# A value path on unscaled rows for the first block of a spectral filter with a gated MLP

## The chip, the cores and the metric

The kernel runs on one core of one Trainium2 chip. The metric is the device time of one execution in microseconds. Before the change, the median of 5 runs is 895.74 us (894.26 to 896.88).

## The reference

```python
def _attn_ref(x, filt_r, filt_i):          # x: 8 x 3008 x 256
    X = np.fft.rfft(x, axis=1)
    Y = X * (filt_r + 1j * filt_i)[None]
    return np.fft.irfft(Y, n=x.shape[1], axis=1)

def _moe_ref(x, w_gate, w_val, w_out, rms_g):   # x: 24064 x 256, hidden width 1536
    rms = np.sqrt(np.mean(x * x, axis=-1, keepdims=True) + 1e-06)
    xn = x / rms * rms_g
    g = xn @ w_gate
    silu = g * (1.0 / (1.0 + np.exp(-g)))
    return silu * (xn @ w_val) @ w_out
```

The first function filters each of the 8 sequences along its length in the frequency domain. The second normalizes every row of the result by its root mean square, multiplies by a gain for each column, and puts it through a gated MLP. Inputs and output are fp32. Row scaling and a matmul on the columns commute: `(x / rms * g) @ w` is `((x * g) @ w) / rms`. That holds for the value product and for the output product, not for the gate, which goes through a nonlinear function.

## The kernel before, in words

The transforms are matmuls with constant tables, in two stages forward and two back. Sequence 0 has its own set-up path (lines 637 to 734), which keeps everything on the chip; sequences 1 to 7 go through DRAM scratch tensors and are interleaved with the MLP of the sequence before.

The MLP works in blocks of 512 rows: 6 blocks for each of 8 sequences, and for each block 12 steps over the hidden width in slices of 128. One step is a slot. `gv` (line 429) runs four 128x512 matmuls: two halves of the contraction (dt 0 and 1) for the gate into `pg`, two for the value into `pv`. ScalarE makes `sg`, the Silu of `pg`; VectorE multiplies `pv` by it into `hh`. `down`, two slots later, multiplies `hh` by the output weights and accumulates in two PSUM banks, `po0` and `po1`. After the last slice ScalarE copies `po0` and VectorE copies `po1` to the output tile `o3` (lines 465 and 466), which is then stored. `pg` and `pv` have two PSUM buffers each.

The normalized rows `xn` of a block come from a chain. `n_first` (block (0,0)) or `n_unit` (the others) makes the last transform stage `psn`, transposed so that the 256 columns lie in two halves of 128 partitions; `dh` 0 and 1 name the halves. ScalarE squares both into `sq`. `y` is `psn` times the gain: for block (0,0), `y_first` does half 0 on VectorE and half 1 on ScalarE. `q_unit` sums the squares by matmuls with a vector of ones into `psq`; VectorE makes `u` (line 353), and GpSimd raises it to the power -0.5 into `rho`, one number a row. For block (0,0) `scale_split` splits `rho` into two fp16 parts `hl`, and `scale_apply` spreads them over the partitions by matmuls (`psr`) and multiplies `y` by them into `xn` on VectorE, half after half.

Every engine gets its instructions in the order in which the program writes them down, so what waits holds up all that stands behind it on its engine. From line 753 on, a list of slots with functions planned into them is such an order for the whole MLP. Around the change the order is written out by hand:

```python
        first = n_first()
        t2_unit(3, 1, 1)
        t2_unit(4, 1)
        t2_unit(5, 1)
        fill = bank(2, "pw")
        warm_up(2, fill)
        y_first(*first, 1)
        q_unit(0, 0)
        t2_unit(6, 0, 0)
        t2_unit(7, 0)
        warm_up(5, fill)
        y_first(*first, 0)
        scale_split(0, 0)
        scale_apply(0, 0, 3)
```

`t2_unit(j, eng)` is four transposes of data of sequence 0 and their copy out of PSUM, on VectorE where `eng` is 1 and on ScalarE where it is 0; the PSUM bank is shared with the unit two before it where no other is given. `warm_up` runs 128x512 matmuls on zeros whose result nobody reads. `bank(1, ..)` and `bank(2, ..)` take the next buffer of `pg` and of `pv`. The weights are loaded by `w_load` in three parts on GpSimd's queue, two in line 706 and on, the third after the set-up (line 732), ahead of the loads of sequence 1.

Of the kernel before, what the change touches and what calls it, by code (L numbers as in the profile page):

```python
# [10 lines left out]
FP32 = mybir.dt.float32  # L11
FP16 = mybir.dt.float16
AXT = mybir.ActivationFunctionType
ALU = mybir.AluOpType
# [6 lines left out]
P = 128  # L21
# [100 lines left out]
def kernel(  # L122
# [11 lines left out]
    nc = tc.nc  # L134
# [9 lines left out]
    glob = ctx.enter_context(tc.tile_pool(name="glob", bufs=1))  # L144
# [6 lines left out]
    up = ctx.enter_context(tc.tile_pool(name="up", bufs=2))  # L151
    xnp = ctx.enter_context(tc.tile_pool(name="xnp", bufs=4))
    hp = ctx.enter_context(tc.tile_pool(name="hp", bufs=4))
    psG = ctx.enter_context(tc.tile_pool(name="psG", bufs=2, space=bass.MemoryType.PSUM))
    psV = ctx.enter_context(tc.tile_pool(name="psV", bufs=2, space=bass.MemoryType.PSUM))
# [11 lines left out]
    wg = glob.tile([P, 2, DFF], FP16)  # L167
    wv = glob.tile([P, 2, DFF], FP16)
    wo = glob.tile([P, JT, D], FP16)
    gsb = glob.tile([P, 2], FP32)  # L170
    hhs = [glob.tile([P, 512], FP16, name="hh%d" % i) for i in range(4)]
    ones = glob.tile([P, 1], FP16)
    mhalf = glob.tile([P, 4], FP32)


    st = {b: {"x": {}, "t1": {}, "t2": {}, "s": {}, "t3": {}, "t4": {}, "y": {}, "sq": {},
# [14 lines left out]
    def bank(i, name):  # L191

        pool, tag = ((psM, "mx"), (psG, "pg"), (psV, "pv"), (psB, "mb"), (psO, "po1"), (psO, "po0"))[i]
        return pool.tile([P, 512], FP32, tag=tag, name=name)
# [114 lines left out]
    def nq(b, m):  # L309
        return 3 if (m == 5 and b % 2 == 0) else 4  # L310
# [24 lines left out]
    def halved(b, m):  # L335
        return b > 1 and (b, m) != (2, 0)
# [5 lines left out]
    def q_unit(b, m):  # L342
        sq = st[b]["sq"].pop(m)
        ps = bank(1, "psq")
        n = nq(b, m)
        parts = 1 if halved(b, m) else 2
        for q in range(n):
            for dh in range(parts):
                nc.tensor.matmul(ps[:, q:q + 1], sq[:, dh, ts(q, P)], ones,  # L349
                                 start=(dh == 0), stop=(dh == parts - 1))  # L350
        u = up.tile([P, 4], FP32, tag="u", name="u")
        rho = up.tile([P, 4], FP32, tag="rho", name="rho")
        nc.vector.tensor_scalar(out=u[:, 0:n], in0=ps[:, 0:n], scalar1=1.0 / D, scalar2=1e-6 * Y_SCALE * Y_SCALE,  # L353
                                op0=ALU.mult, op1=ALU.add)
        nc.gpsimd.tensor_tensor(out=rho[:, 0:n], in0=u[:, 0:n], in1=mhalf[:, 0:n], op=ALU.pow)  # L355
        if (b, m) not in by_matmul:
            nc.gpsimd.dma_start(r_d[b, m, 0:n * P].rearrange("(p q) -> p q", q=n), rho[:, 0:n])
        else:
            st[b]["u"][m] = rho
# [7 lines left out]
    def n_first():  # L367

        y = yp.tile([P, 2, 512], FP32, tag="y", name="y")
        sq = sqp.tile([P, 2, 512], FP16, tag="sq", name="sq")  # L370
        pss = [bank(1 + dh, "psn") for dh in range(2)]
        for dh in range(2):
            for q in range(4):
                nc.tensor.matmul(pss[dh][:, ts(q, P)], st[0]["t4"][0][:, q, ds(dh * P, P)], wai,
                                 start=True, stop=True)
            nc.scalar.activation(out=sq[:, dh, :], in_=pss[dh], func=AXT.Square)
        st[0]["sq"][0] = sq
        st[0]["y"][0] = y
        return y, pss

    def y_first(y, pss, dh):
        if dh:
            nc.scalar.activation(out=y[:, dh, :], in_=pss[dh], func=AXT.Identity, scale=gsb[:, dh:dh + 1])
            return
        nc.vector.tensor_scalar(out=y[:, dh, :], in0=pss[dh], scalar1=gsb[:, dh:dh + 1],
                                scalar2=None, op0=ALU.mult)

    def scale_split(b, m):
        rho = st[b]["u"].pop(m)
        hl = up.tile([P, 2, 4], FP16, tag="hl", name="hl")  # L390
        nc.vector.tensor_copy(out=hl[:, 0, :], in_=rho)
        nc.vector.tensor_tensor(out=hl[:, 1, :], in0=rho, in1=hl[:, 0, :], op=ALU.subtract)
        st[b]["u"][m] = hl
# [26 lines left out]

    by_matmul = ((0, 0), (0, 1), (1, 0))
    hh_of = {}
    po_of = {}
    late_p = {}

    def cut(b, m, part):
        return (0, nq(b, m)) if part is None else (2 * part, 2)

    def gv(b, m, jt, part):
        q0, n = cut(b, m, part)  # L430
        w = n * P
        xn = st[b]["xn"][m][:, :, q0 * P:q0 * P + w]
        pg = psG.tile([P, 512], FP32, tag="pg", name="pg")
        pv = psV.tile([P, 512], FP32, tag="pv", name="pv")
        order = [(e, dt_) for e in range(2) for dt_ in range(2)]
        if (b, m, jt) == (0, 0, 0):
            order = [(e, dt_) for dt_ in range(2) for e in range(2)]
        for e, dt_ in order:
            ps, wt = ((pg, wg), (pv, wv))[e]
            nc.tensor.matmul(ps[:, 0:w], wt[:, dt_, ts(jt, P)], xn[:, dt_, :],  # L440
                             start=(dt_ == 0), stop=(dt_ == 1))
        sg = hp.tile([P, 512], FP16, tag="sg", name="sg")
        hh = hhs[(6 * JT * b + JT * (m + (part or 0)) + jt) % 4]
        nc.scalar.activation(out=sg[:, 0:w], in_=pg[:, 0:w], func=AXT.Silu)  # L444
        nc.vector.tensor_tensor(out=hh[:, 0:w], in0=pv[:, 0:w], in1=sg[:, 0:w], op=ALU.mult)  # L445
        hh_of[(b, m, jt, part)] = hh

    def down(b, m, jt, part):
        hh = hh_of.pop((b, m, jt, part))
        if jt == 0:  # L450
            where = {None: ((psO, "po0"), (psO, "po1")), 0: ((psO, "po0"),), 1: ((psO, "po1"), (psM, "mx"))}
            po_of[(b, m, part)] = [pool.tile([P, 2, D], FP32, tag=tag, name=tag)
                                   for pool, tag in where[part]]
        po = po_of[(b, m, part)]

        n = cut(b, m, part)[1]
        per = 1 if part else 2
        for s4 in range(n):
            nc.tensor.matmul(po[s4 // per][:, s4 % per, :], hh[:, ts(s4, P)], wo[:, jt, :],  # L459
                             start=(jt == 0 and s4 % per == 0),  # L460
                             stop=(jt == JT - 1 and (s4 % per == per - 1 or s4 == n - 1)))
        if jt == JT - 1:
            o3 = late_p["op"].tile([P, 4, D], FP32, tag="o3", name="o3")
            if part is None:
                nc.scalar.activation(out=o3[:, 0:2, :], in_=po[0], func=AXT.Copy)
                nc.vector.tensor_copy(out=o3[:, 2:n, :], in_=po[1][:, 0:n - 2, :])  # L466
            else:
                nc.scalar.activation(out=o3[:, 0, :], in_=po[0][:, 0, :], func=AXT.Copy)
                nc.vector.tensor_copy(out=o3[:, 1, :], in_=po[part][:, 1 - part, :])
            po_of[(b, m, part)] = o3  # L470
# [105 lines left out]
    def t2_unit(j, eng, bk=None):  # L576
        c, r = divmod(2 * j, XC)
        if r == 0:
            st[0]["t4"][c] = t4p.tile([P, XC, D], FP16, tag="t4", name="t4")
        pool, tag = (psO, "po%d" % (j % 2)) if bk is None else ((psM, "mx"), (psB, "mb"))[bk]  # L580
        ps = pool.tile([P, 2, D], FP16, tag=tag, name="pt2")
        for a in range(2):
            for dh in range(2):
                src = gT[:, dh, :].rearrange("p (i n) -> p n i", n=H)[:, 2 * j + a, :]
                nc.tensor.transpose(ps[:, a, ts(dh, P)], src, ident)  # L585
        dst = st[0]["t4"][c][:, r:r + 2, :]
        if eng:
            nc.vector.tensor_copy(out=dst, in_=ps)
        else:
            nc.scalar.activation(out=dst, in_=ps, func=AXT.Copy)  # L590
# [20 lines left out]
    def warm_up(n, pw):  # L611
        if isinstance(pw, int):
            pw = bank(pw, "pw")
        for i in range(n):
            nc.tensor.matmul(pw, wz[:, 0:P], wz, start=True, stop=True)
# [5 lines left out]

    def w_load(q):
        cols = ts(q, DFF // 3)
        for src, dst in ((moe_w_gate, wg), (moe_w_val, wv)):
            nc.gpsimd.dma_start(dst[:, :, cols], src.rearrange("(dt p) j -> p dt j", p=P)[:, :, cols])
        nc.gpsimd.dma_start(wo[:, ts(q, JT // 3), :],
                            moe_w_out.rearrange("(jt p) d -> p jt d", p=P)[:, ts(q, JT // 3), :])

    with tc.manual_schedule():
# [84 lines left out]
        t2_unit(2, 1, 0)  # L714
        first = n_first()
        t2_unit(3, 1, 1)
        t2_unit(4, 1)
        t2_unit(5, 1)
        fill = bank(2, "pw")
        warm_up(2, fill)  # L720
        y_first(*first, 1)
        q_unit(0, 0)
        t2_unit(6, 0, 0)
        t2_unit(7, 0)
        warm_up(5, fill)
        y_first(*first, 0)
        scale_split(0, 0)
        scale_apply(0, 0, 3)
        t2_unit(8, 0)
# [147 lines left out]
```

## Time and profile before

| what | value |
|---|---|
| median of 5 runs | 895.74 us (894.26 to 896.88) |
| the profiled execution | 893.84 us, span of its instructions 892.1 us |
| TensorE busy | 874.7 us (98%), granted clock 1.00 |
| VectorE, ScalarE, GpSimd busy | 677.2, 623.9, 428.6 us |
| first gate matmul | 47.74 us after the span's start |
| last slice of block (0,0) accumulated, copies begin | 69.92 us |

The median belongs to plain runs, the rows of the profile to one profiled execution, which has a time of its own. Busy time of TensorE is counted to the modelled end of each matmul, and neighbours overlap, so a busy TensorE may still have small waits in it. In a timeline a row gives the start, the length, the engine, the line of the kernel and what is written from what; rows of one kind that follow each other are merged.

### The profile page before, as it was taken

To read this page: it belongs to the slowest core of one execution; us is meant where nothing else is said; L and a number is where in the kernel's file an instruction comes from. 1 tells how busy PE (TensorE), PEld (TensorE's weight loads), DVE (VectorE), ACT (ScalarE), POOL (GpSimd) and SP (SyncE) were. 2 spreads that over 40 slices of the span, in tenths; PEclk is the share of its full clock that TensorE was granted. 3 is DMA by queue.
4 is the path that set the end of the run, shared out by engine and by line. 5 is a ranking of instruction groups with operands and counts; after the bars stand their busy time and mean duration, and the time that the engine had idled before them with its cause. 6 is when DMAs were issued, how large, how long until landed. Compare 5 with 4: busy or idle time off the path is not lost.

```text
span 892.1 us, 17504 instructions
## 1 busy us (share of the span) xinstructions
PE 874.7 (98%) x6289; PEld 561.3 (63%) x6289; DVE 677.2 (76%) x1085; ACT 623.9 (70%) x1063; POOL 428.6 (48%) x385
## 2 busy tenths in 40 slices
PE   8799999999999999999999999999999999999997
PEld 5666666666666666666666666666666666666556
DVE  7866766889988887888688786888878887555555
ACT  7877666677677766877677766787657765676444
POOL 7843720656437652577236662376515762155300
PEclk9999999999999999999999999999999999999999
DMA  9595826674653446434645347332352232221301
GB/s 199 109 205 155 157 61 202 142 161 114 155 159 98 101 101 186 116 86 117 152 125 127 87 84 199 80 103 83 84 165 72 66 89 60 87 67 48 72 24 48
DMA packets 80094, 101.43 MB, mean 114 GB/s; under 512 B 8108, under 2 KB 56684, under 8 KB 79560
## 3 DMA queue, kind: packets, MB, share of 16 engines
q1 hardware_dynamic: 69688, 84.23, 34.6%
q0 software_dynamic: 10240, 15.96, 11.2%
q8 instruction: 49, 0.80, 0.4%
q14 instruction: 37, 0.30, 0.1%
q10 hardware_dynamic: 80, 0.13, 0.1%
HBM read 67.67 MB, written 46.78 MB: 128 GB/s over the span
## 4 chain that ended last, share of the span: by engine, by line
PE 91%; DVE 3%; issue 2%; POOL 1%; DMA 1%; ACT 1%; POOLq 0%; DVEq 0%
PE po L459 27%; PE pg L440 26%; PE pv L440 26%; PE psb L238 3%; PE psi L288 3%; PE psn L320 2%; PE psa L203 2%; DMA xc<-in_x_dram 1%; DVE o L466 1%; DVE hh L445 1%; PE psq L349 1%; POOL xc L188 0%; PE pt L546 0%; POOL xn L416 0%; PE pt L585 0%
## 5 line engine op out<-in xcount | busy, mean ns | idle before, releaser
L445 DVE TENSOR_TENSOR hh<-pv,sg 128x512 f16<-128x512 f32 (+2 forms) x588 | 393.3, 670 | 195.4 <-ACT sg L444 82.9
L444 ACT ACTIVATE sg<-pg 128x512 f16<-128x512 f32 (+2 forms) x588 | 341.0, 580 | 226.6 <-PE pg L440 217.8
L459 PE MATMUL po<-wo,hh 128*128 128x256 f16 x2244 | 343.1, 272 | 2.9 <-DVE o L466 2.2
L440 PE MATMUL pg<-xn,wg 128*128 128x512 f16 (+2 forms) x1176 | 339.6, 370 | 0.1
L440 PE MATMUL pv<-xn,wv 128*128 128x512 f16 (+2 forms) x1176 | 339.6, 370 | 0.0
L459 PEld LDWEIGHTS <-hh 128*128 128x128 f16 x2256 | 216.3, 98 | 98.0 <-issue 4.3
L279 POOL TENSOR_TENSOR s<-s,s 128x512 f16<-128x512 f16 x96 | 111.1, 1157 | 230.8 <-DVE s L273 159.6
L440 PEld LDWEIGHTS <-wv 128*128 128x128 f16 x1176 | 114.8, 98 | 128.8 <-issue 0.3
L416 POOL TENSOR_TENSOR xn<-y,rb 128x1024 f16<-128x1024 f32 (+1 forms) x45 | 126.1, 2803 | 44.0 <-DMA rb<-r_tmp 41.0
L440 PEld LDWEIGHTS <-wg 128*128 128x128 f16 x1176 | 111.3, 98 | 13.2 <-issue 0.6
L355 POOL TENSOR_TENSOR rho<-u,mhalf 128x4 f32<-128x4 f32 (+1 forms) x48 | 49.0, 1021 | 63.1 <-DVE u L353 62.6
L293 ACT ACTIVATE t<-psi 96x512 f16<-96x512 f32 x112 | 66.4, 593 | 9.4 <-PE psi L288 4.3
L326 ACT ACTIVATE y<-psn,gsb 128x512 f32<-128x512 f32 (+1 forms) x94 | 63.8, 679 | 8.1 <-PE psn L320 0.9
L273 DVE TENSOR_TENSOR s<-psb,fi 64x512 f16<-64x512 f32 x96 | 65.7, 684 | 3.0
L275 DVE SCALAR_TENSOR_TENSOR s<-psb,fi 64x512 f16<-64x512 f32 x96 | 66.5, 693 | 1.3
L249 DVE TENSOR_TENSOR s<-psb,fr 128x512 f16<-128x512 f32 x96 | 65.4, 681 | 0.0
L340 POOL TENSOR_TENSOR sq<-sq 128x512 f16<-128x512 f16 (+1 forms) x35 | 39.7, 1133 | 34.3 <-ACT sq L332 34.3
L332 ACT ACTIVATE sq<-psn 128x512 f16<-128x512 f32 (+1 forms) x94 | 54.8, 582 | 0.0
L208 ACT ACTIVATE t<-psa 128x512 f16<-128x512 f32 x70 | 41.8, 597 | 5.6 <-PE psa L203 2.4
L288 PE MATMUL psi<-s,wi 128*128 128x256 f16 x248 | 45.4, 273 | 0.0
L238 PE MATMUL psb<-t,wb 96*128 96x256 f16 x224 | 43.0, 272 | 0.7 <-DVE s L266 0.7
L320 PEld LDWEIGHTS <-t 128*128 128x128 f16 x368 | 28.4, 98 | 20.6 <-issue 0.4
(106 smaller groups left out, 533.6 us busy)
## 6 DMA issues: line engine op xcount, KB each, us to landing
out_dram<-o SPq DMA_DIRECT2D x83, 256.0 KB
xc<-in_x_dram POOLq DMA_DIRECT2D x56, 192.0 KB, 6.1
z_tmp<-t SPq DMA_DIRECT2D x28, 384.0 KB
t<-z_tmp SPq DMA_DIRECT2D x28, 384.0 KB
g_tmp<-t SPq DMA_DIRECT2D x56, 192.0 KB
rb<-r_tmp SPq DMA_DIRECT2D x41, 256.0 KB
t<-g_tmp SPq DMA_DIRECT2D x21, 384.0 KB
t<-g_tmp SPq DMA_DIRECT2D x7, 320.0 KB
```

The lines of the kernel that those rows point to most:

```text
L238: nc.tensor.matmul(ps[:, u, :], w[:, k, :], t, start=True, stop=True)
L249: nc.vector.tensor_tensor(out=s1, in0=ps, in1=f1, op=ALU.mult)
L273: nc.vector.tensor_tensor(out=s2[a], in0=ps[e], in1=f2[e], op=ALU.mult)
L275: nc.vector.scalar_tensor_tensor(out=s2[a], in0=ps[e], scalar=-1.0, in1=f2[e], op0=ALU.mult, op1=ALU.mult)
L279: nc.gpsimd.tensor_tensor(out=s, in0=s1, in1=s2, op=ALU.add)
L288: nc.tensor.matmul(ps[:, u, :], wi_at(q, 2 * i + u), ss[q][:, u, :], start=(q == 0), stop=(q == n - 1))
L293: nc.scalar.activation(out=st[b]["t3"][c][:, 2 * r:2 * r + 2, :], in_=ps[0:KR], func=AXT.Copy)
L416: nc.gpsimd.tensor_tensor(out=xv, in0=yv, in1=rv.unsqueeze(1).to_broadcast([P, 2, n, P]), op=ALU.mult)
L440: nc.tensor.matmul(ps[:, 0:w], wt[:, dt_, ts(jt, P)], xn[:, dt_, :], start=(dt_ == 0), stop=(dt_ == 1))
L444: nc.scalar.activation(out=sg[:, 0:w], in_=pg[:, 0:w], func=AXT.Silu)
L445: nc.vector.tensor_tensor(out=hh[:, 0:w], in0=pv[:, 0:w], in1=sg[:, 0:w], op=ALU.mult)
L459: nc.tensor.matmul(po[s4 // per][:, s4 % per, :], hh[:, ts(s4, P)], wo[:, jt, :], start=(jt == 0 and s4 % per == 0), stop=(jt == JT - 1 an ...
```

## The change

Block (0,0)'s value product is made from rows that carry the gain but not yet the row scale, in fp16 (`y16`). Its first two slices are multiplied ahead of the row scale, in the place of the warm-up matmuls. The gate still uses `xn`. The row scale `rho`, kept in a tile of its own, is applied where block (0,0)'s output leaves PSUM, in two operations of 256 columns on ScalarE and two on VectorE. The value weights are loaded before the gate weights.

```diff
-        rho = up.tile([P, 4], FP32, tag="rho", name="rho")
+        rho = up.tile([P, 4], FP32, tag="rho", name="rho") if (b, m) != (0, 0) else rho0
...
+        y16.append(xnp.tile([P, 2, 512], FP16, tag="xn", name="y16"))
...
+    def val_first(jt):
+        pv = psV.tile([P, 512], FP32, tag="pv", name="pv")
+        for dt_ in (1, 0):
+            nc.tensor.matmul(pv, wv[:, dt_, ts(jt, P)], y16[0][:, dt_, :], start=(dt_ == 1), stop=(dt_ == 0))
+        pv_of[jt] = pv
...
-        pv = psV.tile([P, 512], FP32, tag="pv", name="pv")
-        order = [(e, dt_) for e in range(2) for dt_ in range(2)]
-        if (b, m, jt) == (0, 0, 0):
-            order = [(e, dt_) for dt_ in range(2) for e in range(2)]
-        for e, dt_ in order:
-            ps, wt = ((pg, wg), (pv, wv))[e]
-            nc.tensor.matmul(ps[:, 0:w], wt[:, dt_, ts(jt, P)], xn[:, dt_, :],
-                             start=(dt_ == 0), stop=(dt_ == 1))
+        pv = pv_of.pop(jt) if (b, m) == (0, 0) and jt < 2 else None
+        if pv is None:
+            pv = psV.tile([P, 512], FP32, tag="pv", name="pv")
+            operands = ((pg, wg, xn), (pv, wv, y16[0] if (b, m) == (0, 0) else xn))
+        else:
+            operands = ((pg, wg, xn),)
+        for ps, wt, src in operands:
+            for dt_ in range(2):
+                nc.tensor.matmul(ps[:, 0:w], wt[:, dt_, ts(jt, P)], src[:, dt_, :],
+                                 start=(dt_ == 0), stop=(dt_ == 1))
...
-            if part is None:
+            if (b, m) == (0, 0):
+                for q in range(4):
+                    src = po[q // 2][:, q % 2, :]
+                    if q < 2:
+                        nc.scalar.activation(out=o3[:, q, :], in_=src, func=AXT.Copy, scale=rho0[:, q:q + 1])
+                    else:
+                        nc.vector.tensor_scalar(out=o3[:, q, :], in0=src, scalar1=rho0[:, q:q + 1],
+                                                scalar2=None, op0=ALU.mult)
+            elif part is None:
...
-        for src, dst in ((moe_w_gate, wg), (moe_w_val, wv)):
+        for src, dst in ((moe_w_val, wv), (moe_w_gate, wg)):
...
         t2_unit(3, 1, 1)
+        y_first(y16[0], first[1], 0)
         t2_unit(4, 1)
         t2_unit(5, 1)
-        fill = bank(2, "pw")
-        warm_up(2, fill)
+        y_first(y16[0], first[1], 1)
+        q_unit(0, 0)
+        y_first(*first, 0)
         y_first(*first, 1)
-        q_unit(0, 0)
         t2_unit(6, 0, 0)
         t2_unit(7, 0)
-        warm_up(5, fill)
-        y_first(*first, 0)
+        val_first(0)
+        val_first(1)
         scale_split(0, 0)
         scale_apply(0, 0, 3)
```

## The prediction

> **What bounds the kernel now.** First the page: busy time and the chain that ended last.
>
> ```profile
> PE 874.7 (98%) x6289; PEld 561.3 (63%) x6289; DVE 677.2 (76%) x1085; ACT 623.9 (70%) x1063; POOL 428.6 (48%) x385
> ...
> PE 91%; DVE 3%; issue 2%; POOL 1%; DMA 1%; ACT 1%; POOLq 0%; DVEq 0%
> ```
>
> TensorE sets the time almost everywhere, so a microsecond of it counts where it has no wait to hide in. The change touches only 43 to 52 us and the end of block (0,0), near 70 us. So I read the timelines of the first stretch: TensorE, then VectorE, then ScalarE (columns: start us, length us, work).
>
> ```profile
> 43.83 0.59 PE L615 MATMUL pw<-wz 128*128 128x512 f16 x2
> 44.26 0.34 PE L349 MATMUL psq<-ones,sq 128*128 128x1 f16 x8
> 44.47 0.75 PE L585 MATMUL pt<-tb,gT 128*128 128x128 f16 x8
> 45.05 1.24 PE L615 MATMUL pw<-wz 128*128 128x512 f16 x5
> 46.20 0.76 PE L401 MATMUL psr<-tb,hl 128*128 128x128 f16 x8
> 46.80 1.00 PE L585 MATMUL pt<-tb,gT 128*128 128x128 f16 x12
> 47.74 0.38 PE L440 MATMUL pg<-xn,wg 128*128 128x512 f16 x1
> ```
> ```profile
> 43.47 1.09 DVE L588 COPY t<-pt 128x512 f16<-128x512 f16 x3 [0.77 <-PE pt L585]
> 44.64 0.16 DVE L353 TENSOR_SCALAR u<-psq 128x4 f32<-128x4 f32 x1
> 44.72 0.74 DVE L385 TENSOR_SCALAR y<-psn,gsb 128x512 f32<-128x512 f32 x1
> 45.97 0.17 DVE L391 CAST hl<-rho 128x4 f16<-128x4 f32 x1 [0.51 <-POOL rho L355]
> 46.18 0.16 DVE L392 TENSOR_TENSOR hl<-rho,hl 128x4 f16<-128x4 f32 x1
> ...
> 47.00 1.29 DVE L405 TENSOR_TENSOR xn<-psr,y 128x512 f16<-128x512 f32 x2 [0.66 <-PE psr L401]
> ```
> ```profile
> 48.81 0.60 ACT L444 ACTIVATE sg<-pg 128x512 f16<-128x512 f32 x1 [0.45 <-PE pg L440]
> 49.54 0.69 ACT L326 ACTIVATE y<-psn,gsb 128x512 f32<-128x512 f32 x1
> 50.13 0.59 ACT L444 ACTIVATE sg<-pg 128x512 f16<-128x512 f32 x1
> 50.61 0.60 ACT L332 ACTIVATE sq<-psn 128x512 f16<-128x512 f32 x1
> ```
>
> The seven warm-ups (pw, 0.216 us each: 5 from 45.05 end where the next could start at 46.13) fill time in which the row scale is made: u at 44.64, rho on GpSimd 44.89 to 45.94, hl to 46.34, psr, xn, and 47.74 for the first gate matmul. That serial chain, 3.1 us from u, sets the start of block (0,0), not the warm-ups. Then ScalarE's sg, y, sq run back to back, and the psn matmuls of the next block wait for sq's end (51.21) until 51.26. From there to 69.90 TensorE is busy 18.40 of 18.40 us: what has moved at 51.26 stays moved.
>
> **What the Trainium skill says.** *TensorE: Matmul & The Clock Gate*, Part 2 (step-by-step): matmuls stay in program order, only weight loads are pulled ahead. So the four early value matmuls stand in front of psr and could hold it up; the chain above, u to psr to pg, is such an order. The same page, Part 1: the clock halves after an idle window of some 3.4 us. Here it is 1.00 even over the emptiest stretch of that length after the first 20 us that I found:
>
> ```profile
> 36.90:40.30 3.40, 1.82 (x39) 1.55 (x37) 1.69 (x3) 1.63 (x5) 3.40 (x4) 1.00 0.00 0
> ```
>
> (TensorE busy 1.82 of 3.40 us, clock 1.00.) *ScalarE: Activation LUTs*, "What ACT_TABLE_LOAD costs": 186 ns + 0.833 ns an element, about 93 ns more for each per-partition operand, about 93 ns of overlap back to back. The trace agrees within 20 ns: 591 to 597 ns for a 128x512 copy, 384 for 128x256, 688 for 128x512 with a gain.
>
> **The change, part by part.**
>
> *Warm-ups out.* 7 x 0.216 = 1.51 us of TensorE, all inside waits. The first two delay psq: sq ends at 44.05, so psq could run at 44.10 instead of 44.26. That 0.16 us gains nothing, because of the next part. Counted 0.
>
> *Two y16 operations in.* The ScalarE half (like y, 0.69) goes in ahead of y: y's half ends near 45.35 and the two transposed copies behind it near 46.4; wanted by xn at 48 and by transposes at 47.5. Hidden; without that cover 0.59. The VectorE half stands between the copies of transposes 3 and 4, ahead of u. Queue: copy at 43.47, y16 at 43.81, which holds it 0.61 (the start-to-start step of such an operation: xn's two take 1.29 for 2, one lasts 0.69), then copies at 44.42 and 44.75, then u at 45.09. Before it was 44.64, there held by psq (the three copies end at 44.56). So u is **0.45 late**, and behind u: rho, the third weight load and x loads on GpSimd's queue, hl, psr, xn. xn's first half ends at 48.14, pg at 48.19.
>
> *Four value matmuls ahead of psr.* 4 x 0.216 = 0.86 us. Transpose 7 waits for copy 5 to free its bank: 45.22; the value matmuls run 45.50 to 46.37; psr's hl comes at 46.65. They fit with 0.28 to spare. In the old place they cost: the first two were interleaved with the gate's while xn's second half was made, the other two followed.
>
> *Block (0,0)'s start, new.* First gate pair 48.19 and 48.79 (xn halves are 0.60 apart), done 49.17. Transpose 11 49.00, psn 49.28 to 49.50, second gate pair to 49.93, third to 50.36 (its bank is free when sg ends, 49.86). ScalarE: sg 49.26 (before 48.81), y when psn is done, 49.76 (before 49.54), then sg 50.35 and sq 50.83 to 51.43. Third value pair: waits for hh of the first, 49.89 + 0.69 = 50.58, so 50.63 to 51.06. Next psn: 51.48, against 51.26. So of 0.45 lost, the moved matmuls give back 0.23: **+0.22 us**. The four matmuls are worth little because ScalarE's four operations, not TensorE, set this stretch.
>
> *Output copy of block (0,0).*
>
> ```profile
> 69.92 0.59 ACT L465 ACTIVATE o<-po 128x512 f32<-128x512 f32 x1
> ...
> 70.62 0.68 DVE L466 COPY o<-po 128x512 f32<-128x512 f32 x1
> ```
> ```profile
> 70.96 0.77 PE L459 MATMUL po<-wo,hh 128*128 128x256 f16 x4
> ```
>
> Those four matmuls take 0.77 where four others take 0.60: the second pair waits for the VectorE copy to end (71.30). The new form is two 128x256 operations with a row scale. VectorE: a 128x256 copy is 0.42, a gain adds 0.06 (0.74 against 0.68), and one follows after 0.40: 0.40 + 0.48 = 0.88 for 0.68, **+0.20 us**, all on that wait. ScalarE: 0.38 + 0.09 = 0.48, the second 0.38 after the first: 0.86 for 0.59; ends 70.78, ahead of 70.96, and the next sg at 70.68 feeds hh at 71.4, which is wanted at 72.65. Hidden (without cover, 0.27).
>
> *Weight loads reordered.* Value before gate. The first landings were 4.3 us after 38.99 and 4.8 after 39.78. So value weights land at 43.3 (wanted 45.5), gate weights at 44.6 (wanted 48.2). The second slices land by 51.2 and are wanted from 53.2, the third by 55.5 and from 59.1. The x loads behind a rho 0.45 later stand in a queue whose engines are saturated to 61 us; the first lands near 59.9 and is wanted at 60.37 plus the shift. Counted 0; at worst 0.45.
>
> *y16's buffer* is held to the end of block (0,0); the fourth xn after it comes some 14 slots later. 0. Removed from TensorE over the whole program: only the warm-ups.
>
> Sum: 0.22 + 0.20 = +0.42 us. On the profiled execution, 893.84 (span 892.1 and 1.7 around it) becomes 894.26; that execution was 1.9 below the median of the runs, so the same step on 895.74 gives **896.2**. Bounds: y16 on VectorE may cost 0.34 (like a copy) to 0.74 (nothing overlapped), the output copy 0 to 0.5: +0.1 to +1.0.
>
> **Rivals.** (a) *The TensorE work really leaves the path*: 0.86 for the moved matmuls, up to 2.37 with the warm-ups. For it: TensorE is 91% of the chain, and the chain even names pw at 45.22. Against: pw ends where hl ends. 893.4 to 894.9. (b) *The clock drops*: without warm-ups, 44.6 to 48.0 holds about 2.5 us of work in 3.4, half of it transposes; a halved clock for one such window costs 1.7: 897.9. It decides once activity falls under what 36.9 to 40.3 shows, or if transposes don't count. That is the case on the slower side. (c) *A new wait in front of psr*: the value matmuls wait for their weights, which were not needed until 47.96. From a landing at 45.8 on, each us late is a us lost; at the 6.1 us of the third load in place of 4.3, 45.1, still in time. 896.5 to 897.5. (d) *Waits elsewhere shift*: the five VectorE-to-po stalls (2.2 us in all) and three psb ones (0.7) change with phase: +0.5 to +2.
>
> **Numbers.** Forecast (+0.1 to +1.0) 0.58, (a) 0.10, (b) 0.10, (c) 0.07, (d) 0.15. No change means within 0.2%, 1.8 us, about what a measurement here can tell. (b), half of (c) and (d), and a little scatter are slower: 0.24; the bottom of (a) faster: 0.06; same 0.70. The runs before spread 894.3 to 896.9, so a median may stand some 0.7 off; the range reaches to the top of (a) and past (b): 894.7 to 898.4. The likeliest case alone: 895.4 to 897.2.
>
> **What would show it.** u at 45.1, with y16 just ahead of the copies of transposes 4 and 5; first pg near 48.2; the four early pv between 45.5 and 46.4; psn near 51.5; the po matmuls after block (0,0) at 0.97 instead of 0.77; clock 1.00. I am wrong if u is not late, if pg starts before 47.7, if psr waits for TensorE, or if the stretch after 51.5 runs differently.

## The result, and the profile after

| | median | lowest to highest | runs |
|---|---|---|---|
| before | 896.55 us | 893.31 to 901.38 | 78 |
| changed | 898.38 us | 894.33 to 905.25 | 43 |

The medians differ by 1.8 us; the ratio on record, 1.0024 (1.0015 to 1.0033), is 2.2 us (1.3 to 3.0) of 896.55. The changed kernel is slower, where +0.4 was forecast. Both kernels spread over more than the difference. The ratios below leave out two runs that took 3243 and 983 us. The profiled execution of the changed kernel took 896.77 us, span 894.7.

The page of the changed kernel, busy times and the chain that ended last:

```profile
PE 874.0 (98%) x6282; PEld 560.8 (63%) x6282; DVE 677.8 (76%) x1087; ACT 624.0 (70%) x1065; POOL 428.2 (48%) x385
...
PE 89%; DVE 4%; DMA 3%; issue 2%; POOL 1%; ACT 1%; ACTq 0%; POOLq 0%
```

TensorE lost the seven warm-ups and nothing else. In the chain a transfer's share rises from 1% to 3%; that is the first hint. The timelines of the stretch that was changed, TensorE, VectorE and ScalarE of the changed kernel:

```profile
45.31 0.43 PE L604 MATMUL pt<-tb,gT 128*128 128x128 f16 x4 [0.50 <-DVE t L607]
45.58 1.03 PE L393 MATMUL pv<-y,wv 128*128 128x512 f16 x4
46.72 0.76 PE L409 MATMUL psr<-tb,hl 128*128 128x128 f16 x8
...
48.27 0.38 PE L451 MATMUL pg<-xn,wg 128*128 128x512 f16 x1
48.87 0.38 PE L451 MATMUL pg<-xn,wg 128*128 128x512 f16 x1 [0.22 <-DVE xn L413]
...
51.57 0.38 PE L321 MATMUL psn<-tb,t 128*128 128x128 f16 x4 [0.27 <-ACT sq L333]
```
```profile
43.85 0.74 DVE L387 TENSOR_SCALAR y<-psn,gsb 128x512 f16<-128x512 f32 x1
44.51 0.75 DVE L607 COPY t<-pt 128x512 f16<-128x512 f16 x2
45.17 0.15 DVE L354 TENSOR_SCALAR u<-psq 128x4 f32<-128x4 f32 x1
```
```profile
49.34 0.60 ACT L455 ACTIVATE sg<-pg 128x512 f16<-128x512 f32 x1 [0.45 <-PE pg L451]
49.86 0.69 ACT L327 ACTIVATE y<-psn,gsb 128x512 f32<-128x512 f32 x1
50.44 0.59 ACT L455 ACTIVATE sg<-pg 128x512 f16<-128x512 f32 x1
50.92 0.60 ACT L333 ACTIVATE sq<-psn 128x512 f16<-128x512 f32 x1
```

Each of these stands within 0.1 us of where the prediction has it: `u` 45.17 (45.09), `psr` 46.72 (46.65), the first gate matmuls 48.27 and 48.87 (48.19, 48.79), `psn` 51.57 (51.48). `u` is 0.53 late, `psn` 0.31; 0.05 of both was there ahead of the stretch that was changed, as the first set-up transposes show (TensorE; before, changed):

```profile
41.18 1.05 PE L585 MATMUL pt<-tb,gT 128*128 128x128 f16 x12 [0.15 <-ACT gT L569]
```
```profile
41.23 1.04 PE L604 MATMUL pt<-tb,gT 128*128 128x128 f16 x12 [0.15 <-ACT gT L588]
```

The end of block (0,0), too, is as forecast:

```profile
71.27 0.38 PE L470 MATMUL po<-wo,hh 128*128 128x256 f16 x2
71.85 0.38 PE L470 MATMUL po<-wo,hh 128*128 128x256 f16 x2 [0.20 <-DVE o L481]
```

The second pair waits 0.20 us for the output copy. Behind it the Silus of block 1 start 0.45, then 0.50 us later than before, again with 0.05 from the late set-up. Up to there the sum of 0.42 is right, and it is steady: counted from those transposes, which start anywhere from 40.47 to 41.85 us in the seven traces of the two kernels as they are, the Silus of block (0,0), from the second on, are 0.26 us later (0.27 in one) in all three traces of the changed kernel and 0.00 to 0.01 off in all four of the kernel before, and the output copy adds 0.18 to 0.19 in all three.

From there to the end of block 2 nothing changes; then one step of 2.03 us comes at once. ScalarE and TensorE of the changed kernel, near 110 us:

```profile
110.80 0.59 ACT L294 ACTIVATE t<-psi 96x512 f16<-96x512 f32 x1 [2.42 <-DMA g_tmp<-t]
111.29 0.58 ACT L264 ACTIVATE v<-psb 128x512 f32<-128x512 f32 x1
```
```profile
111.93 0.38 PE L239 MATMUL psb<-t,wb 96*128 96x256 f16 x2 [1.80 <-ACT v L264]
```

The same work in the profile before has no such wait:

```profile
108.15 0.59 ACT L293 ACTIVATE t<-psi 96x512 f16<-96x512 f32 x1 [0.27 <-PE psi L288]
108.64 0.58 ACT L263 ACTIVATE v<-psb 128x512 f32<-128x512 f32 x1
```

ScalarE copies a chunk of sequence 1's transform into a buffer (`t3`, of which there are two) that can be written only when an earlier chunk has been stored to DRAM. It stands 2.42 us in that wait; `v` behind it in its queue is late, `v` keeps a PSUM bank, and TensorE waits 1.80 us for that bank. Why the store is late is seen on SyncE's queue of the changed kernel (columns: issue, length, transfer):

```profile
101.17 0.33 SPq L365 DMA_DIRECT2D rb<-r_tmp  x1
101.60 1.00 SPq L219 DMA_DIRECT2D t<-z_tmp  x1
102.69 0.68 SPq L297 DMA_DIRECT2D g_tmp<-t  x1
```

The store (`g_tmp`) stands behind the load of a row scale, which waits for that scale to arrive in DRAM, and behind a load of sequence data. It is issued at 102.69 and the buffer is free at 110.80, 8.1 us later. The same queue before (the last row merges two stores, the first of them issued at 101.56):

```profile
100.67 0.33 SPq L364 DMA_DIRECT2D rb<-r_tmp  x1
101.09 0.38 SPq L218 DMA_DIRECT2D t<-z_tmp  x1
101.56 4.25 SPq L296 DMA_DIRECT2D g_tmp<-t  x2
```

There the buffer was free 6.6 us later or sooner, at 108.15, and nobody waited for it.

A third difference lies at the very end. The last Silus, before and changed:

```profile
886.55 0.38 ACT L444 ACTIVATE sg<-pg 128x256 f16<-128x256 f32 x1 [0.27 <-PE pg L440]
```
```profile
888.95 0.38 ACT L455 ACTIVATE sg<-pg 128x256 f16<-128x256 f32 x1 [0.27 <-PE pg L451]
```

From there to the end of the span it is 5.51 us before and 5.74 in the changed kernel, and the time on record is longer than the span by 1.78 us before and by 2.09 in the changed kernel. Together that is 0.54 us, and it is as steady as the path: 5.51 to 5.53 us in every trace of the kernel before and of its variants below against 5.73 to 5.78 in those of the changed kernel (the one of 3243 us apart), and, in every execution with a span on record, 1.72 to 1.85 us outside the span for the former against 2.04 to 2.17 for the latter, of which there are 196. What in the change brings it, no run tells. It isn't the warm-ups or the weight order alone: e2 and f2 don't have it, e3 has it in both parts and f1 outside the span.

So the trace of the changed kernel shows +0.45 from the change's own path, +0.54 at the program's end, and +2.0 from a wait 40 us after the path that the change doesn't touch. Does the change bring that wait, or does the kernel before have it too, with a profiled execution that happened to be without it? The latter is my theory; rivals are a halved clock, the lost warm-ups and the order of the weights.

### The profile page after: what moved, and what is told of

It is laid out like the page before. It is cut to its first block, busy times and chain, and to the rows that moved or that the text cites. A ratio compares the mean times of both kernels' runs of the same rounds, so it can differ in the third digit from the quotient of the medians.

```text
span 894.7 us, 17494 instructions
## 1 busy us (share of the span) xinstructions
PE 874.0 (98%) x6282; PEld 560.8 (63%) x6282; DVE 677.8 (76%) x1087; ACT 624.0 (70%) x1065; POOL 428.2 (48%) x385
## 4 chain that ended last, share of the span: by engine, by line
PE 89%; DVE 4%; DMA 3%; issue 2%; POOL 1%; ACT 1%; ACTq 0%; POOLq 0%
PE po L470 26%; PE pg L451 26%; PE pv L451 26%; PE psi L289 3%; PE psb L239 3%; PE psn L321 2%; PE psa L204 2%; DMA fr<-in_filt_r_dram 1%; DMA g_tmp<-t 1%; DVE o L485 1%; DVE hh L456 1%; DVE fr L676 1%; DMA fi<-in_filt_i_dram 1%; PE psq L350 1%; ACT sg L455 0%
## 5 line engine op out<-in xcount | busy, mean ns | idle before, releaser
L451 PE MATMUL pv<-xn,wv 128*128 128x512 f16 (+2 forms) x1152 | 332.3, 370 | 0.0
```

The lines of the kernel that those rows point to most:

```text
L451: nc.tensor.matmul(ps[:, 0:w], wt[:, dt_, ts(jt, P)], src[:, dt_, :], start=(dt_ == 0), stop=(dt_ == 1))
```

## The experiments

A trace has 588 Silus. The steps named below are jumps in their delay, that is, in the start of each against the same one in the profile before. The kernel before ran beside each group; its medians were 897.66 us (67 runs, with the e kernels), 898.42 (59, f) and 897.84 (59, g).

**The changed kernel again** (e1, h4), without an edit.

> The changed kernel unaltered, for its clock in several executions and a second trace. Its first trace is 0.5 us behind the kernel before at 73 us, as the sum of the prediction says, and 2.5 us behind from 109 us on, where ScalarE waits for a store to DRAM. Clock theory (TensorE is granted half its clock for one or more windows of about 3.4 us in some executions, since the warm-ups are gone): ratio to before 1.001 to 1.003, granted clock at or below 0.998 in a good part of the executions, and a trace that has the 109 us wait or not without it mattering. Store theory (the wait at 109 us comes with the changed order and is most of the loss): the wait of about 2 us is in the second trace too, and the clock is like that of the kernel before.

> The changed kernel, unaltered, a third execution. Theory (it meets the store wait in most executions): 2 to 3 us of idle time on ScalarE ahead of its copy of the transposed values near 110 us, 897 to 898.5 us. Rival (the wait is as rare in it as in the kernel before): no such wait, and 894.5 to 895.5 us.

Measured: 898.40 us in 22 runs, ratio 0.9995 (0.9977 to 1.0014), beside 1.0024 above: on this chip the kernels can't be told apart. The two intervals just miss each other, so the loss may not be of the same size on every occasion. Its profiled execution, 898.33 us, has 0.6 us on TensorE for x at 61 us and the wait for the store again, 2.35 us on ScalarE. The third execution took 898.92 us:

```profile
112.92 0.59 ACT L294 ACTIVATE t<-psi 96x512 f16<-96x512 f32 x1 [4.05 <-DMA g_tmp<-t]
```

The wait is in all three executions of the changed kernel, 2.42, 2.35 and 4.05 us, and it isn't of one size; the third is larger than expected.

**The kernel before again** (h1 to h3), three more executions.

> The kernel before, unaltered, looked at once more. Theory (its recorded execution had the set-up's transfers land well, and others of its executions wait at the same two places as the changed kernel): a DMA wait of 1 to 3 us near 61 us (x or rho of the next rows) or near 109 us (the store that frees the transposed buffer) in at least one of three such looks; where there is one, the time is 895.5 to 898. Rival (the changed kernel alone runs into the store wait): none near 109 us in any look, and times near 894 to 895.

> As the look before it: a DMA wait near 61 or near 109 us in at least one of three looks if the kernel before meets them too; none near 109 us in any of them if the change alone brings it.

> As the two looks before it: a DMA wait near 61 or near 109 us in at least one of three looks if the kernel before meets them too; none near 109 us in any of them if the change alone brings it.

Measured: 897.29, 897.46 and 893.80 us. ScalarE near 110 us in the first, the second and the third:

```profile
110.79 0.59 ACT L293 ACTIVATE t<-psi 96x512 f16<-96x512 f32 x1 [3.06 <-DMA g_tmp<-t]
```
```profile
110.76 0.59 ACT L293 ACTIVATE t<-psi 96x512 f16<-96x512 f32 x1 [3.50 <-DMA g_tmp<-t]
```
```profile
107.92 0.59 ACT L293 ACTIVATE t<-psi 96x512 f16<-96x512 f32 x1 [0.75 <-DMA g_tmp<-t]
```

So the change isn't needed for the wait: the kernel before, unaltered, stands in it in three of four executions, and in two of them for longer than the changed kernel did in its first profile. The two with a long wait took 897.3 and 897.5 us, the two others 893.8. The profile that the prediction was made from is of the second kind, 2.7 us below the median of 78 runs. The rival, that only the changed kernel runs into the wait, falls, and so does the order of the weights as its cause, since this kernel loads the gate first. Whether the change makes the wait longer or more frequent is another question; it comes back below.

**Before without its seven warm-ups** (e2): both `warm_up` calls out.

```diff
-        warm_up(2, fill)
...
-        warm_up(5, fill)
```

> The kernel before with only its seven warm-up matmuls at 43.8 and 45.05 us left out. Clock theory: slower than before by about as much as the changed kernel, 1 to 3 us, with clocks below 0.999 in more of the executions. Store theory: within 0.5 us of before, since psr waits for hl and psq for the VectorE queue either way; psq runs at 44.1 and u at 44.6 as before.

Measured: 897.15 us, ratio 1.0003 (0.9990 to 1.0017). The first Silu starts 0.05 us from where it was; counted from the set-up's transposes (41.40 here) it is 0.18 earlier, since `psq` no longer stands behind two warm-ups. The warm-ups carried nothing, as counted. But this trace has two waits of its own, 1.4 us at 61 us and 1.3 at 109 (TensorE, in the view of waits):

```profile
PE psr L401 <- DVE hl L391: 1.4, 1, 1.4
PE psb L238 <- ACT v L263: 1.3, 1, 1.3
```

The first of them comes from GpSimd's queue (columns: start, length; idle time before and what ended it):

```profile
59.68 0.52 POOL L188 DMA_DIRECT2D xc<-in_x_dram  x1 [3.92 <-DMA wo<-in_moe_w_out_dram]
60.27 1.03 POOL L355 TENSOR_TENSOR rho<-u,mhalf 128x4 f32<-128x4 f32 x1
```

The last x load can't be issued until the third output-weight load has landed, 3.92 us; the row scale `rho` of block 1 stands behind it on that queue, and `hl` and `psr` behind `rho`. In the profile before the same wait was 1.32 us and `rho` began at 56.40. This is a second place where the set-up's backlog of transfers decides.

**The changed kernel with five warm-ups put back** (e3) into its two waits (two ahead of `q_unit`, three ahead of `t2_unit(7, 0)`).

```diff
+        fill = bank(3, "pw")
+        warm_up(2, fill)
         q_unit(0, 0)
...
+        warm_up(3, fill)
         t2_unit(7, 0)
```

> The changed kernel with five warm-up matmuls put where TensorE waits: two ahead of psq, three between transposes 6 and 7. None of them is on the path: psr still waits for hl at 46.7, the first gate matmul is at 48.3. Clock theory: the loss falls to the 0.4 to 0.6 us of the prediction's sum, ratio 1.000 to 1.001. Store theory: no change against the changed kernel, ratio 1.001 to 1.003, and a wait of about 2 us near 109 us.

Measured: 899.70 us, ratio 1.0023 (1.0006 to 1.0040). Filling the gaps recovers nothing (the unaltered changed kernel beside it had 0.9995); the store's wait is there, 3.1 us.

**The changed kernel with `u` first** (e4): the VectorE half of `y16` behind `q_unit` instead of ahead of it.

```diff
-        y_first(y16[0], first[1], 0)
         t2_unit(4, 1)
...
         q_unit(0, 0)
+        y_first(y16[0], first[1], 0)
```

> The changed kernel with the VectorE half of y16 behind u in place of ahead of it. By the prediction's sum u comes back to about 44.65, the first gate matmul to about 47.8, and the psn matmuls of the next block to about 51.0 (0.5 us earlier than in the changed kernel); the value matmuls then wait for y16 until about 45.4 and psr follows them at 46.3. Path theory: 0.5 us less than the changed kernel. Clock theory: that too, but most of the loss of 1 to 3 us stays. Store theory: the wait at 109 us may go, since everything is 0.5 us earlier, and then the loss goes with it.

Measured: 899.14 us, ratio 1.0019 (1.0004 to 1.0035). VectorE's timeline:

```profile
44.75 0.16 DVE L354 TENSOR_SCALAR u<-psq 128x4 f32<-128x4 f32 x1
44.83 1.41 DVE L387 TENSOR_SCALAR y<-psn,gsb 128x512 f16<-128x512 f32 x2
```

`u` comes back to 44.75, and the Silus of block (0,0) run 0.04 us *earlier* than before instead of 0.31 later. Counted from the set-up's transposes (41.46 here) they are 0.32 earlier instead of 0.26 later, and g4 below, with the same edit, has 0.33. So the late `u` was the path's cost, as the prediction said, and without it the path of block (0,0) is faster than before. The time didn't follow: this execution lost 1.66 us at 61 us and 3.04 at 109. A gain of 0.6 us can't be seen beside waits that move by 2 to 3.

**The order of the weight loads**, alone: back to gate first in the changed kernel (f1), and value first in the kernel before (f2). f2's edit is the change's own swap in `w_load`, f1's its reverse:

```diff
-        for src, dst in ((moe_w_val, wv), (moe_w_gate, wg)):
+        for src, dst in ((moe_w_gate, wg), (moe_w_val, wv)):
```

> The changed kernel with the gate weights loaded first again, as before. Order theory (value weights first disturb the loads behind them, and so the DMA waits near 61 and 109 us): the loss against before shrinks to the 0.5 us of the path, ratio 1.0000 to 1.0008. Backlog theory (the waits near 61 and 109 us are the set-up's backlog of transfers, come in some executions of either kernel and owe nothing to the weight order): as the changed kernel, ratio 1.000 to 1.002, with waits at 61 or 109 us of 0 to 3 us in its trace.

> The kernel before with the value weights loaded first and nothing else changed. Order theory: slower by 1 to 2 us, with the wait at 109 us in its trace. Backlog theory: within 0.6 us of before (ratio 0.9993 to 1.0007), with such waits in its trace as likely as in any other; the first slot's matmuls then wait for no weights, since gate weights land at 44.6 and are wanted at 47.7.

Measured: f1 899.29 us, ratio 1.0009 (0.9997 to 1.0021); f2 897.60, ratio 0.9994 (0.9975 to 1.0013). Neither end of the swap moves the time measurably, though both intervals still allow about 1 us. (f1's one profiled execution is the one of 3243 us and isn't read.) In f2's trace the row scale of block 1 is late again, a step of 1.83 us at 61 us, and there is no wait for the store.

**Taking the backlog away from both kernels** (f3 before, f4 changed). If those waits are what moves the time, both kernels must become faster, and steadier, when the transfers get slack. The first x load goes ahead of the third weights, the last one behind block 1's row scale; the row-scale load of block (0,5), with the `xn` made from it, and one sequence load go to later slots, so the store stands in front of them. In the kernel before:

```diff
+        x_load(1, 0)
         w_load(2)
-        for c in range(NXC):
-            x_load(1, c)
+        x_load(1, 1)
+        x_load(1, 2)
...
+        at(5, x_load, 1, 3)
...
-            norm_plan(0, m, s0, s0 + 2, (2, 5, 8))
+            norm_plan(0, m, s0, s0 + 2, (2, 5, 8) if m < 5 else (2, 9, 12))
...
-... if c < 3 else b_at[4] + 1,
+... if c < 3 else b_at[4] + (5 if b == 1 else 1),
```

> The kernel before with slack given to the transfers: the first x loads of sequence 1 ahead of the third weight part, its last ones after the second row scale on GpSimd's queue, and on SyncE's queue the first stores of sequence 1 ahead of one scratch load and one row-scale load. Backlog theory: the waits near 61 and 109 us are gone or under 0.5 us in its trace, and it is 1 to 2.5 us faster than before, ratio 0.997 to 0.999, since the median execution of the kernel before has these waits too. Order theory: no change against before, since before did not have them.

> The changed kernel with the same slack. Backlog theory: slower than the kernel before with slack by the path's 0.5 us and no more (0 to 1 us), so ratio to before 0.9975 to 0.9995; the two waits gone or under 0.5 us in its trace. Order theory: it falls to the loss of the path too, but the kernel before with slack does not gain, so ratio near 1.0005.

Measured: the kernel before with slack 894.76 us, ratio 0.9967 (0.9952 to 0.9982); the changed kernel with slack 895.67, ratio 0.9978 (0.9969 to 0.9988). The 22 runs of the latter lie between 894.56 and 897.51, and 13 of the 14 of the former between 893.05 and 896.38 (the other is the run of 983), where the kernel before beside them spread from 894.27 to 904.28. That the kernel before gains too is what the order of the weights can't explain. In both traces the wait at 109 us is gone; in the first:

```profile
108.63 0.59 ACT L293 ACTIVATE t<-psi 96x512 f16<-96x512 f32 x1 [0.27 <-PE psi L288]
```

The changed kernel got one new wait, 0.9 us at 60 us for the third gate weights, which now come after the value weights and an x load:

```profile
PE pg L451 <- DMA wg<-in_moe_w_gate_dram: 0.9, 1, 0.9
```

**Only the two SyncE moves** (the last two edits above), in the kernel before (g1) and in the changed one (g2).

> The kernel before with only SyncE's order changed: the row-scale load of block (0,5) and one scratch load of sequence 1 stand behind the first stores of sequence 1. If the store wait near 109 us is the larger part of what a typical execution of before loses, 1 to 2 us faster than before, ratio 0.998 to 0.999; if the waits near 61 us are, 0 to 0.7 us faster. Its trace has no wait near 109 us and may have one of 0 to 2 us near 61.

> The changed kernel with the same change to SyncE's order. If what the changed kernel loses beyond the path's 0.5 us lies in the store wait near 109 us (all of its four traces so far have it, with 2 to 3 us; one of three traces of kernels like before does), it comes to within 0.5 us of the kernel before with the same order, and gains 1.5 to 2.5 us on the changed kernel: ratio to before 0.9985 to 0.9998. If the excess lies elsewhere, it stays 1 to 2 us behind the kernel before with this order.

Measured: before 895.14 us, ratio 0.9978 (0.9967 to 0.9988); changed 896.06, ratio 0.9984 (0.9964 to 1.0004). Neither trace has the store's wait. For the kernel before that alone is worth 2.0 us by the ratio (1.1 to 3.0), 2.7 by the medians. The changed kernel with it comes out ahead of the unaltered kernel before, by 1.4 us, but its interval reaches to no difference; behind g1 it is by 0.9 us, more than the 0.5 expected.

**The full slack in the changed kernel, with the third weights gate first** (g3), and with `u` first on top (g4).

```diff
-        for src, dst in ((moe_w_val, wv), (moe_w_gate, wg)):
+        for src, dst in ((moe_w_val, wv), (moe_w_gate, wg))[::-1 if q == 2 else 1]:
```

> The changed kernel with full slack, and the third weight part in the order gate, value. The trace with full slack alone waited 0.9 us near 60 us for the third gate weights, which came after the value weights. That wait should go: 0.3 to 0.9 us faster than with full slack alone, and 0.5 us slower than the kernel before with full slack; ratio to before 0.9968 to 0.998.

> The same with the VectorE half of y16 behind u as well. The path's loss shrinks to the 0.15 to 0.2 us of the output copy: level with the kernel before with full slack, ratio 0.996 to 0.9977. If it is not below the run beside it, the delay of u was not part of the loss.

Measured: g3 895.99 us, ratio 0.9987 (0.9974 to 1.0001); g4 895.38, ratio 0.9978 (0.9964 to 0.9991). In g3's trace the wait for the gate weights is gone, but the gain expected from that isn't there: f4 had 0.9978. The 0.6 us between g3 and g4 is of the size of the late `u`, but the intervals overlap. None of the changed kernels comes out below f3, the kernel before with slack, though the intervals of g4 and f3 overlap; f3 is 3 us faster than the kernel before beside it (0.0033 times 898).

## Why the prediction was wrong

The forecast was 896.2 us on a median of 895.74, +0.05%, with "no change" likeliest; measured is +0.24%, slower by a little more than its bound of 0.2%. The range, 894.7 to 898.4, reaches just to the measured 898.38, whose level also holds 0.8 us by which the median before came out higher in 78 runs than in 5. That it reaches so far is luck: its upper end was made for a clock drop that didn't come.

Point by point:

- *`u` late by 0.45, +0.22 on `psn`*: right. In the trace 0.53 and 0.31, of which 0.05 is the late set-up; with `u` first the loss is gone. The 0.23 that the moved matmuls were to give back is there both ways: from the first Silu of the block to the later ones the delay falls by 0.22, from 0.53 to 0.31 in the changed kernel and from 0.17 to -0.04 with `u` first (e4).
- *Four value matmuls ahead of `psr`, hidden*: right, 45.58 to 46.61 by the modelled ends, `psr` at 46.72 waits for `hl`. Rival (c) falls.
- *Output copy, +0.20 on VectorE, ScalarE's hidden*: right, 0.20 on the second `po` pair; the Silus behind are later by 0.19, in two steps of 0.14 and 0.05.
- *Warm-ups 0, weight order 0*: right within what e2, f1 and f2 can tell. The gate weights landed at 45.79 us, not at 44.6, still ahead of 48.27. Rival (a) falls with e2.
- *The clock* (b): fell. With five warm-ups back the time stays, no trace of the changed kernel or its variants that is read has a half-clock stretch between 40 and 60 us, and the mean granted clock of the executions with the e kernels is the same for both kernels, 0.998. Half-clock stretches do occur, in both; see the last section.
- *"The change touches only 43 to 52 us and the end of block (0,0)"*, and with it *"893.84 (span 892.1 and 1.7 around it) becomes 894.26"*: this is the first step that failed. The end of the program was carried over unchanged. It costs 0.54 us more, 0.23 in the span and 0.31 around it, in the trace of the changed kernel, and much the same in the others. That is more than the whole forecast of 0.42.
- *"The x loads ... Counted 0; at worst 0.45"*, and nothing at all for the stores behind them: this is the second step that failed, together with *"the same step on 895.74 gives 896.2"*. It took every later wait, and its absence, from one execution and carried them over unchanged. The trace before had a store issued at 101.56, whose buffer was taken at 108.15, and three more executions of that kernel show waits of 0.75, 3.06 and 3.50 us for it. A term that ranges over 3.5 us in the kernel before stood in the sum as zero with a bound of 0.45. Rival (d) named waits that shift elsewhere, at +0.5 to +2 and 0.15, but pinned it on VectorE's `po` and `psb` stalls, which sum to the same in both traces (2.2 and 0.7 us); the wait that decided was ScalarE's, for a transfer.
- *"591 to 597 ns", "within 20 ns"* for ScalarE's copies: the lowest mean of a 128x512 copy on record is 592 ns, and the largest difference is 20.5 ns. Nothing hangs on it.

How much of the loss, 1.8 us by the medians and 2.2 by the ratio, is what? Path and program end make 0.45 + 0.54 = 0.99 us. With the store's wait taken away from both kernels the changed one is behind by 0.9 us twice (895.67 against 894.76, 896.06 against 895.14). That fits the sum, though the intervals also allow less, down to 0, and f4 holds its new weight wait too. The rest, about 1 us, is a matter of how often and how long each kernel waits for the store: 0, 3.06, 3.50 and 0.75 us in four executions before, mean 1.8; 2.42, 2.35 and 4.05 in three after, mean 2.9. The difference of 1.1 would close the sum, but seven executions with this scatter don't show it. That the change makes the wait longer stays open. One thing speaks for it: the row scale stored to DRAM near 81 us lands 3.3 to 3.4 us after its issue in all four executions before and 4.9 to 5.0 in all three after, and in the variants the two kinds stay apart (up to 4.0 us in those of the kernel before, 4.4 and more in those of the changed one). Why, no run here tells, and the issue of the store later on doesn't follow it evenly.

## What to carry to other kernels

A profiled execution that lies at the low end of its kernel's runs (here 893.84 against a median of 896) is telling you what it lacks: before forecasting from it, list the transfers that landed with little margin, and price their waits from a second execution. A change of half a microsecond can't be read against such waits; give the transfers slack in both kernels first, then compare. Compare two traces to their very end, and the time outside the span too: half a microsecond of this change's cost lies there, after all the work it touches. And look at what stands ahead of a store on its queue: moving two loads behind it was worth about 2 us here, more than the 0.86 us of the matmuls that the change moved.

## What the runs showed that I had not expected

**The clock follows windows of 3.41 us on a fixed grid, and a half-empty one can be enough.** The second profile of the kernel before (h1), in stretches of that length (columns: stretch, its length, busy TensorE, weight loads, VectorE, ScalarE, GpSimd; granted clock, share of the DMA engines, GB/s):

```profile
105.94:109.35 3.41, 3.41 (x24) 2.16 (x23) 1.83 (x3) 1.09 (x2) 0.65 (x1) 1.00 1.01 241
109.35:112.76 3.41, 0.98 (x8) 0.68 (x7) 0.37 (x1) 1.77 (x4) 2.15 (x2) 1.00 0.13 36
112.76:116.18 3.42, 3.42 (x13) 1.82 (x12) 2.71 (x5) 1.58 (x3) 1.68 (x2) 0.50 0.07 16
```

The store's wait leaves TensorE busy for 0.98 of 3.41 us, at full clock; the *next* 3.41 us run at half clock although TensorE is busy throughout. The Silus behind lose another 0.84 us. h2 does the same (1.37 busy, then half clock). The half-clock stretches of one execution start a whole number of windows apart: in e3 at 27.10, 115.85 and 897.50, 26 and 229 windows of 3.413. From one execution to the next the grid lies elsewhere. That the window runs freely and is 3413 ns long is what the Trainium skill says (*TensorE: Matmul & The Clock Gate*, Part 1); it speaks of an idle window, and these traces show that a window doesn't have to be idle for it. Ahead of the kernel's last microseconds, in the traces that are read, full clock gave way to half after windows with 0.98, 1.26, 1.37, 1.49, 1.59 and 1.74 us of busy TensorE, and never after one with 1.80 or more that was itself at full clock; windows with 1.55 and 1.69, and one with 1.76 in the first 8 us of h2, were followed by full clock. So in these traces the edge lies near half a window, between about 1.5 and 1.8 us, and busy time by modelled ends doesn't settle it more closely. (The way back isn't as plain: in e3 a second half-clock window follows one in which TensorE was busy for 2.89 us.)

The prediction took 36.9 to 40.3 us, busy 1.82 at clock 1.00, as proof of room. It read the clock in the wrong window, and stood near the edge. In g1 the grid fell otherwise:

```profile
36.63:40.04 3.41, 1.74 (x30) 1.43 (x28) 2.64 (x5) 2.17 (x6) 2.72 (x3) 1.00 0.00 0
40.04:43.45 3.41, 3.41 (x37) 2.85 (x35) 0.56 (x1) 1.36 (x3) 3.41 (x5) 0.50 0.66 82
```

and its first Silu came 1.95 us later than in the profile before. The 43 to 47 us that lost the warm-ups are well clear: the emptiest grid window there in a trace of the changed kernel holds 2.65 us of TensorE.

**One store of 192 KB took from 6.6 us or less to 9.9 us** from its issue to the release of its buffer, in seven executions of the two kernels that issue it at nearly the same point (101.2 to 103.4 us). With the half-clock stretches behind it, it makes nearly all of the 3.5 us between the executions of the kernel before at 893.8 and those at 897.4.
